# A retention layer and a two-layer MLP on one core: seven products also for block 5, and the whole order written down

## The chip, the core and the metric

The kernel runs on one core of a Trainium2 chip. A core has a matrix engine (TensorE, PE in the profile; PEld is its loading of weights), a vector engine (VectorE, DVE), a scalar engine with function tables (ScalarE, ACT), GpSimd (POOL) and SyncE (SP). Each takes its instructions in the order in which the program lists them and waits on semaphores for the others. Sixteen DMA engines move data; here POOL starts the loads, and SP starts the transposes of q and k and most stores. The metric is device time in microseconds (us) of one launch, the median of several runs; lower is better.

## The reference

```python
# q, k, v: (8 batches, 8 heads, 576 positions, 64)
scores = (1 / sqrt(64)) * q @ k.T
gamma  = 1 - 2.0 ** (-5 - arange(8))               # one per head
Dmat   = where(rel >= 0, gamma ** rel, 0)          # rel = query position - key position
x      = ((scores * Dmat) @ v)                     # no softmax
x      = x as (4608 tokens, 512 = heads * 64)
h      = x @ w_in                                  # (512, 2048)
g      = 0.5 * h * (1 + erf(h / sqrt(2)))          # exact gelu
out    = g @ w_out                                 # (2048, 512), float32
```

Products are made in bf16 with float32 sums.

## The kernel before

**Attention.** The work is cut into 36 units. A unit is 128 tokens: 128 positions (a chunk) of one batch with all heads, or, for the last 64 positions, both batches of a pair together. Units of one chunk and both batches of a pair form a group. There are 22 groups, numbered from 0: groups 0 to 3 are units 0 to 3, group 4 is units 4 and 5, group 5 is 6 and 7, group 6 is 8 and 9, group 7 is unit 10 (a short one), group 8 is 11 and 12, and so on. For each unit q, k and v are loaded by POOL (`load`, L322, which casts to bf16 on the way). q and k are turned: for groups 0 to 6 on TensorE (`turn`, L505), from group 7 on by DMA transposes from SP (`turn_dma`, L515). Then come the scores within the chunk (`scores`, L539, L548, L561), their masking on VectorE (`masked`), the product with v (`inner`, L636, L650), the running state of keys and values of earlier chunks (`state`, L669), the queries' product with that state (`cross`, L703), and the copy of the result, scaled by the decay, into the tile x of its block (`evacuate`). `scaled_v` scales v by its decay, on VectorE or ScalarE. These matmuls use halves and quarters of TensorE's array.

**MLP.** A block is 512 tokens, four units; there are nine, 0 to 8. In the first product (`mlp1`, L762) a block needs, for each of 16 slices of d_ff, four matmuls of 128x512. Gelu follows on ScalarE. Blocks 6 to 8 (`FAST = 6`) make the first product another way: `fast` (L1027) takes the 2 by 2 blocks of w_in and x and makes seven products of half size in place of eight (Winograd's form of Strassen's scheme). For each of four parts j of d_ff there are the products P1, P7, P6, P2, P5, P4, P3, each of four matmuls 128x256. They use sums of blocks of w_in (`sum_in`, `sum_last`; the latter writes over w_in, so only after the last plain `mlp1`), differences of blocks of x (`sum_x`), and results that are copied out of PSUM and added again on VectorE or ScalarE between the products: P6 and P2 need P1's copy, P5 and P4 need P6's sum, P3 needs P5's sum. The second product is plain in block 0 (`mlp2`, L807) and of seven products in blocks 1 to 8 (`part`, L946: M3, M4, M5, M1, M2, M6, M7, each in four steps, with the sums of gelu's result made by `sum_g` and those of w_out by `sum_w`).

**Order.** Everything is issued from one Python program, so the order of its calls is the order on each engine. A loop makes it. It keeps an estimate `T` of when each engine is free, and of when each load lands. At each turn it calls `fire`, which issues loads from the list `ORDER`, sums, casts, transposes and scaled v as their estimated times come. Then it chooses the next work for TensorE: cross product and evacuation, state, scores with the products that wait, a turn, or MLP work from `mlp_pick`. The rules are greedy: whatever is ready first. Entries of `ORDER` such as `s11+6` or `p31+20` shift the moment of single actions. While the loop has nothing for TensorE in the first 16 us, it issues filler matmuls on zeros (`warm`, L1241).

```python
        due = [a for a in acts if a[0] <= now]
        ...
        if pick and pick[0] <= now:
            one = pick[1].pop(0)
            ...
            {"1": mlp1, "2": mlp2, "3": part, "4": fast}[one[0]](*one[1:])
```

Copies that may run on either engine go through `either`, which takes the one that the estimate says is done sooner.

Of the kernel before, what the change touches and what calls it, by code (L numbers as in the profile page):

```python
# [9 lines left out]
FP32 = mybir.dt.float32  # L10
# [7 lines left out]
def kernel(  # L18
# [52 lines left out]
    FAST, ALL_FAST = 6, 6  # L71
# [23 lines left out]
    def x_of(i):  # L95
        t = i * C // TOK
        if t not in x_tiles:
            x_tiles[t] = x_pool.tile([128, N_DM, TOK], BF16, tag="xT", name="xT")
        return x_tiles[t][:, :, i * C % TOK:i * C % TOK + C]
# [157 lines left out]
    def sw_dma(issue, kind, put):  # L257
# [31 lines left out]
    def load(what, i):  # L289
# [17 lines left out]
        if what == "wo":  # L307
# [3 lines left out]
            queued.append((land_out[i] + 4.0, 3, sum_w, (i,)))  # L311
            return
        bp, ci, j = units[i]
        qk, v_ld = tiles_of(i)
        src = {"q": q, "k": k, "v": v}[what]
        for jj in (j,) if j is not None else range(2):
# [6 lines left out]
            if j is not None:  # L323
                sw_dma(0.94, "ld", putter(land, (what, i)))
            else:
                sw_dma(0.74, "short", putter(land, (what, i)))

    cast_due = {}
    for x, keys in enumerate(zip(*HW_FIRST)):
        for n, (what, i) in enumerate(keys):  # L330
# [3 lines left out]
    ORDER = ("wi1 k1 wi0 io q1 v0 q2 k2 v1 wi2 v2 k3 wi3 q3 v3 wi4 wi5 wi6 k4 q5 q4 q6 k5 v4 wi7 wo0 dq2 wo1 wo2 "  # L334
# [6 lines left out]
             "u3+0 u4+8 z12+0.3 p28+15 z15+1.6 z19+2.2 b18+4 p30+25 a19 p25+21 z23+2.2 u6+16 z6+0.3").split()  # L341

    BY_ACT = {int(x[1:]) for x in ORDER if x[0] == "a"}
    S_LATE = {int(x[1:].split("+")[0]): float(x.split("+")[1]) for x in ORDER if x[0] == "s"}
    B_LATE = {int(x[1:].split("+")[0]): float(x.split("+")[1]) for x in ORDER if x[0] == "b"}
    DVE_LAG, P_WAIT, HURRY = ({int(x[1:].split("+")[0]): float(x.split("+")[1]) for x in ORDER if x[0] == kind} for kind in "zpu")
    ORDER = [x for x in ORDER if x[0] not in "abszpu"]

    rest = const.tile([128, 2], BF16, name="rest")

    for n, g in enumerate(groups):
        ORDER += [what + str(i) for what in "qkv" for i in g if what + str(i) not in ORDER and (what, i) not in first]

    def v_free(i):
        return "Bdone" in st[i] if i in raw else "V" in st[i]

    def next_order():
        what = ORDER[0].rstrip("0123456789")
        n = int(ORDER[0][len(what):] or 0)
        if what == "h":  # L360
            if n >= nD:
                return False
            nc.gpsimd.tensor_copy(rest, qkT_of(n)[:, :, 0, 0])
            T["pool"] = max(T["pool"], sg[n]["T"]) + 0.2
        elif what in "qkv" and (group_of[n] >= next_load[0] or n >= 4 + N_V and not v_free(n - N_V)):
            return False
        else:
            load(what, n)
        ORDER.pop(0)
        return True  # L370
# [6 lines left out]

    next_load = [group_of[12] + 1]
    nD = N_PE_TR
    while T["pool"] < 4.0:  # L380
        next_order()

# [35 lines left out]
    def pe_waits(until):  # L418
        T["pe"] = max(T["pe"], until)
# [69 lines left out]
    def qkT_of(n):  # L489
        s = sg[n]  # L490
        if "qkT" not in s:
            if n < 4:
# [5 lines left out]
    def turn(n, jj, half):  # L498
# [8 lines left out]
        done = either(0.42 * rows / C, done, qkT[:, jj, HP * half:HP * half + HP, 0:rows], t[:, :, 0:rows])  # L507
# [3 lines left out]
    def turn_dma(n, jj):  # L511
# [10 lines left out]
        hw_dma(1.3, MOVE["turn"] * (0.62 if short else 1.0), max(land["qk"[jj], i] for i in groups[n]), put)  # L522

    def turnable(now):
        if nD >= len(groups) or nD >= group_of[min(nX, N_U - 1)] + N_QKT:
            return None
        return next((jj for jj in range(2) if jj not in sg[nD].get("ends", {})
                     and all(("qk"[jj], i) in land and land["qk"[jj], i] - 0.3 <= now for i in groups[nD])), None)

    def scores(n):  # L530
# [3 lines left out]
        if n < 4:  # L534
# [6 lines left out]
            st[g[0]]["sc"] = got, pe(0.23, H, "row")  # L541
            return
# [20 lines left out]
        done = pe(0.46, 4 * H, "quad")  # L563
        for j, i in enumerate(g):
            st[i]["sc"] = got[j], done

    def masked(i):
# [3 lines left out]
        (got, done) = s.pop("sc")  # L571
        if i < 4:
# [32 lines left out]
    def scaled_v(i):  # L605
# [3 lines left out]
        vh = vh_pool.tile([128, H, D], BF16, tag="vh", name="vh")  # L609
        at = land["v", i]  # L610
        by_act = i in BY_ACT
# [15 lines left out]
    def inner(i):  # L627
        bp, ci, j = units[i]
        s = st[i]
        pe_waits(max(s["R"], s["V"] if "vh" in s and i not in raw else land["v", i]))  # L630
# [22 lines left out]
        s["Bdone"] = True  # L653
        if j is None:
            s_done.add(i)
        elif j == 1 and ci < NCI - 1 and (bp, ci) != (1, 0):
            u_due.append((bp, ci))

    def state(bp, ci):
        pair = pair_of[bp, ci]  # L660
        assert (bp, ci) == (1, 0) or nX > (pair_of[bp, ci - 1] if ci else pair_of[bp - 1, NCI - 2] if bp else [-1])[-1]
# [16 lines left out]
        if pair[0] >= 4 and next_load[0] < len(groups):  # L678
            reload()
# [6 lines left out]

    def reload():
        next_load[0] += 1

    def cross(n):  # L690
# [14 lines left out]
        done = pe(0.2 if j0 is not None else 0.12, 2 * H, "quad")  # L705
        for i in g:
            st[i]["B"] = done

    def evacuate(i):
        bp, ci, j = units[i]  # L710
        s = st[i]
        if i in raw:
# [26 lines left out]
        if j is None and next_load[0] < len(groups):  # L739
            reload()  # L740
# [5 lines left out]

    def g_of(t, mm):
        return g_tiles[t, mm // 2][:, mm % 2] if t else g_tiles[t, mm // 2][mm % 2]

    def g_done(t, j):  # L750
        if t > 0 and all((t, 4 * j + x, ts) in g_at for x in range(4) for ts in range(4)):
            at = max(g_at[t, 4 * j + x, ts] for x in range(4) for ts in range(4)) - SEM
            for x in range(3):
                queued.append((at, x, sum_g, (t, j, x)))

    def mlp1(t, m0, n, lo, hi):
# [15 lines left out]
        done = on("act", 0.17 + n * (hi - lo) * 0.00084, done)  # L772
# [3 lines left out]
        g_done(t, m0 // 4)  # L776
# [23 lines left out]
    def mlp2(t, ts, m0, m1):  # L800
        cols = slice(ts * 128, ts * 128 + 128)
        if m0 == 0:
# [9 lines left out]
        if m1 == N_DF:  # L812
            if ts < 2:
# [25 lines left out]
    def sum_g(t, j, n):  # L839
# [8 lines left out]
        at = on("dve", 0.42 if n == 1 else 0.69, max(begun[x] for x in users_of(t - 1, j, n))) + SEM  # L848
# [7 lines left out]

# [552 lines left out]
```

## Time and profile before

| | |
|---|---|
| median of 3 runs | 286.22 us (286.12 to 286.31) |
| the profiled execution | 285.38 us |
| its span, first to last instruction | 283.6 us |
| TensorE busy | 276.4 us, 97% of the span |
| VectorE, ScalarE, POOL busy | 201.6, 144.2 and 114.2 us |
| granted TensorE clock | 1.0 throughout |
| chain that ended last | 88% TensorE |

A profile shows one execution. Its rows name a line of the kernel, an engine, an operation and tiles (out<-in). Waiting is told as idle time of an engine with the releaser that ended it. The chain is followed back from the last instruction: at each step to what released it, or to the instruction before it on its engine. Some records of matmuls are missing, a few in a hundred at most, so counts of matmuls in a row can be short by one or two.

### The profile page before, as it was taken

Reading aid. Unit: us, or ns where it says so; the run is one execution under the profiler, and the core shown is the slowest. Engines: PE = TensorE matmul, PEld = TensorE weight load, DVE = VectorE, ACT = ScalarE, POOL = GpSimd, SP = SyncE. Lnnn points to the kernel's source line nnn. Section 1 sums busy time; section 2 is a strip of 40 time slices with the busy share of each in tenths; the row PEclk is TensorE's granted clock in tenths of the full one; section 3 lists DMA queues with packets and bytes.
Section 4 is the critical chain, followed back from the end, with each engine's and each line's share of the span. In section 5 each row is a group of like instructions: output and inputs, shape, how many; then the busy total and the mean of one; then the engine's idle time right before and its main releaser. Section 6 shows DMA issues by size and latency. Waiting matters only on the chain.

```text
span 283.6 us, 8015 instructions
## 1 busy us (share of the span) xinstructions
PE 276.4 (97%) x3341; PEld 206.7 (73%) x3359; DVE 201.6 (71%) x395; ACT 144.2 (51%) x301; POOL 114.2 (40%) x143
## 2 busy tenths in 40 slices
PE   7999999999999999999999999999999999999994
PEld 2586577578874588457775687558888888888894
DVE  5743654959576765988549835899888779978732
ACT  5665635545456624696426524566655453545320
POOL 8988997994246484335548553000000000000000
PEclk9999999999999999999999999999999999999999
DMA  9999999999999999999999999960002100400133
GB/s 148 166 182 165 194 175 171 138 125 143 170 171 191 196 144 119 202 190 127 170 184 145 190 132 141 219 84 3 0 2 76 74 2 0 150 1 2 74 113 111
DMA packets 152804, 35.38 MB, mean 125 GB/s; under 512 B 141121, under 2 KB 148929, under 8 KB 152769
## 3 DMA queue, kind: packets, MB, share of 16 engines
q0 software_dynamic: 116832, 18.10, 97.0%
q1 hardware_dynamic: 34528, 16.26, 32.4%
q10 hardware_dynamic: 1408, 0.52, 0.8%
q8 instruction: 26, 0.43, 0.7%
q14 instruction: 10, 0.07, 0.1%
HBM read 36.70 MB, written 9.44 MB: 163 GB/s over the span
## 4 chain that ended last, share of the span: by engine, by line
PE 88%; POOL 6%; DMA 3%; issue 1%; DVE 1%; POOLq 0%
PE psum L946 35%; PE psum L762 26%; PE psum L1027 13%; PE psum L807 5%; DMA qk_ld<-in_q_dram 3%; PE psum L650 3%; PE psum L561 3%; POOL w_in L295 2%; POOL qk L322 2%; PE psum L669 1%; PE psum L703 1%; POOL v_ld L322 1%; PE psum L505 1%; POOL qk_ld L322 1%; PE psum L548 0%
## 5 line engine op out<-in xcount | busy, mean ns | idle before, releaser
L762 PE MATMUL psum<-xT,w_in 128*128 128x512 bf16 (+3 forms) x548 | 86.4, 311 | 1.0 <-issue 0.3
L771 ACT ACTIVATE g<-psum 128x512 bf16<-128x512 f32 (+2 forms) x106 | 58.3, 557 | 37.2 <-PE psum L762 35.4
L762 PEld LDWEIGHTS <-w_in 128*128 128x128 bf16 x560 | 48.5, 98 | 33.6 <-issue 0.5
L946 PEld LDWEIGHTS <-gs 128*128 128x128 bf16 x656 | 62.2, 98 | 7.8
L946 PE MATMUL psum<-w_sum,gs 128*128 128x256 bf16 (+1 forms) x400 | 48.3, 269 | 0.0
L322 POOL DMA_DIRECT2D v_ld<-in_v_dram x40 | 34.0, 858 | 16.6 <-DMA qk_ld<-in_k_dram 10.6
L322 POOL DMA_DIRECT2D qk_ld<-in_q_dram x36 | 30.5, 856 | 22.8 <-DMA qkT<-qk_ld 7.3
L322 POOL DMA_DIRECT2D qk_ld<-in_k_dram x36 | 30.5, 858 | 19.7 <-DMA qk_ld<-in_q_dram 19.4
L946 PE MATMUL psum<-w_out,gs 128*128 128x256 bf16 x256 | 32.7, 273 | 0.0
L946 PE MATMUL psum<-w_sum,g 128*128 128x256 bf16 x256 | 30.3, 273 | 0.0
L946 PEld LDWEIGHTS <-g 128*128 128x128 bf16 x256 | 24.8, 98 | 3.8
L1052 ACT ACTIVATE g<-psum 128x512 bf16<-128x512 f32 x36 | 20.4, 589 | 12.4 <-PE psum L1027 8.3
L593 DVE TENSOR_TENSOR ret<-psum,msk 128x1024 bf16<-128x1024 f32 x15 | 18.0, 1220 | 11.6 <-PE psum L561 4.7
L843 DVE TENSOR_TENSOR gs<-g 128x1024 bf16<-128x1024 bf16 x32 | 21.7, 685 | 5.3 <-ACT g L771 5.0
L847 DVE TENSOR_TENSOR gs<-g 128x1024 bf16<-128x1024 bf16 x32 | 21.4, 683 | 0.0
L1027 PEld LDWEIGHTS <-w_in 128*128 128x128 bf16 x192 | 18.7, 98 | 2.3
L898 DVE SCALAR_TENSOR_TENSOR o<-psum,o 128x512 f32<-128x512 f32 (+1 forms) x9 | 5.6, 630 | 19.4 <-PE psum L946 16.1
L617 DVE TENSOR_TENSOR vh<-v_ld,dv 128x512 bf16<-128x512 bf16 x28 | 18.4, 682 | 0.8 <-DMA v_ld<-in_v_dram 0.8
L484 ACT COPY o<-psum 128x512 f32<-128x512 f32 x13 | 7.6, 585 | 19.1 <-PE psum L946 19.1
L484 ACT CAST u_sb<-psum 128x512 bf16<-128x512 f32 x15 | 8.7, 586 | 15.8 <-PE psum L669 15.8
L614 ACT ACTIVATE vh<-v_ld,dv 128x64 bf16<-128x64 bf16 x64 | 16.1, 337 | 0.0
L1048 ACT ACTIVATE g<-p 128x512 bf16<-128x512 f32 x12 | 7.6, 630 | 16.1 <-DVE p L1046 16.1
(101 smaller groups left out, 357.1 us busy)
## 6 DMA issues: line engine op xcount, KB each, us to landing
out_dram<-o SPq DMA_DIRECT2D x27, 256.0 KB, 6.5
v_ld<-in_v_dram POOLq DMA_DIRECT2D x32, 128.0 KB, 9.8
qk_ld<-in_k_dram POOLq DMA_DIRECT2D x28, 128.0 KB, 9.6
qk_ld<-in_q_dram POOLq DMA_DIRECT2D x28, 128.0 KB, 8.8
w_in<-in_moe_w_in_dram POOLq DMA_DIRECT2D x8, 256.0 KB, 6.8
w_out<-in_moe_w_out_dram POOLq DMA_DIRECT2D x8, 256.0 KB, 7.6
out_dram<-o SPq DMA_DIRECT2D x14, 128.0 KB, 2.3
v_ld<-in_v_dram POOLq DMA_DIRECT2D x8, 64.0 KB, 8.5
```

The costliest lines, as they stand in the source:

```text
L322: nc.gpsimd.dma_start(dst, src[2 * bp + jj, :, ci * C:ci * C + n, :].rearrange("h s d -> s h d"))
L484: nc.scalar.copy(dst, src)
L593: nc.vector.tensor_tensor(r.rearrange("p e h q -> p (e h) q"), both_of(got[0][0], HP), by, op=ALU.mult)
L614: nc.scalar.activation(vh[:, h, :], loaded[i][1][:, h, :], AF.Copy, scale=dv[:, h, ci:ci + 1])
L617: nc.vector.tensor_tensor(vh, loaded[i][1], dv[:, :, ci:ci + 1].to_broadcast([128, H, D]), op=ALU.mult)
L762: nc.tensor.matmul(hT[:, m, :], lhsT=w[:, cc, o:o + 128], rhs=x_tiles[t][:, cc, lo:hi], start=(cc == 0), stop=(cc == N_DM - 1))
L771: nc.scalar.activation(g_of(t, m0 // 2)[:, m0 % 2:m0 % 2 + n, lo:hi], hT, AF.Gelu)
L843: nc.vector.tensor_tensor(s.rearrange("p m a b -> p m (a b)"), g[:, :, 0, :], g[:, :, 1, :], op=ALU.add)
L847: nc.vector.tensor_tensor(s, g[:, :, :, LEFT], g[:, :, :, RIGHT], op=MINUS)
L946: nc.tensor.matmul(m[:, 0 if apart else ts, :], lhsT=a, rhs=w[:, c0:c1], start=p in begins and mm == 0 and ts == 0, stop=mm == N_DF // 2 - ...
L1027: nc.tensor.matmul(m[:, y, :], lhsT=a[:, c], rhs=d[:, c], start=p in (P1, P7) and y == 0 and c == 0, stop=c == 1, skip_group_check=True)
L1052: nc.scalar.activation(g[:, :, rows, cols], m, AF.Gelu)
```

## The change

Blocks 5 to 8 now make the first product with seven products (`FAST = 5`). For blocks 5 and 6 the buffer of P7 is a tile in the place of the table `near` (decay factors, last read when unit 28's scores are masked); for blocks 7 and 8 it stays in a load buffer.

The greedy loop, `fire`, `mlp_pick` and the readiness rules are gone. A list `SEQ` of some 1,100 actions takes their place, each with its arguments: `L3.1` loads w_in1, `s7` makes the scores of group 7, `m10` masks unit 10, `f5.0.1` is block 5, part 0, second product (P7), `p4.3.1` is block 4, fourth of the seven second products, step 1, `G` is `sum_g`, `I`, `J` and `X` are the sums for the seven products, `d7.1` a DMA transpose of k, `v5.1` scaled v on ScalarE. A loop performs them in turn. The list was recorded from a run of such rules and then changed by a search that moves single actions. The estimate `T` still exists: it decides in `either`, and the functions now note more of the times at which buffers come free.

```diff
-    FAST, ALL_FAST = 6, 6
+    FAST, ALL_FAST = 5, 5
...
-    ORDER = ("wi1 k1 wi0 io q1 v0 q2 k2 v1 wi2 v2 k3 wi3 q3 v3 wi4 wi5 wi6 k4 q5 q4 q6 k5 v4 wi7 wo0 dq2 wo1 wo2 "
-             "v5 dq3 wo3 k7 k6 k8 q9 wo5 wo7 dq4 v7 q7 wo4 v6 wo6 k9 q11 v11 q8 v10 q12 k10 v9 v8 q10 k12 k11 v12 "
...
-    def scaled_v(i):
+    def scaled_v(i, by_act):
...
+    near_p7 = True
+    def late_p7(t):
+        return not near_p7 or t >= N_BLK - 2
...
         elif p == P7:
-            if not p7_tiles:
-                p7_tiles.append(ld_pool.tile([128, 2, 2, 256], FP32, tag="qk", bufs=N_LD, name="p7"))
-            f_bank[key, "p7"] = p7_tiles[0][:, j % 2]
-            at = either(0.68, done, f_bank[key, "p7"], m)
+            late = t >= N_BLK - 2
+            if late not in p7_tiles:
+                more = {"tag": "qk", "bufs": N_LD} if late else {"tag": "near"}
+                p7_tiles[late] = (ld_pool if late else const).tile([128, 2, 2, 256], FP32, name="p7", **more)
+            f_bank[key, "p7"] = p7_tiles[late][:, j % 2]
+            at = either(0.68, max(done, p7_free(t, j)), f_bank[key, "p7"], m)
...
-    while True:
-        fire()
-        now = T["pe"]
...
+    SEQ = ("L3.1 L1.1 L3.0 L5.0 L0.1 L2.0 L0.2 L1.2 C0.0 C1.0 t0.0.0 Z0 w2 L2.1 Z0 Z1 t0.1.0 Z0 w5 L3.2 Z1 s0 m0 L2.2 Z1 "
+           "w7 L1.3 Z1 t1.0.0 L3.3 Z1 t1.1.0 w2 Z1 i0 L0.3 Z1 v0.0 x0 e0 w2 s1 m1 L2.3 t2.0.0 10.0.2.0.128 L3.4 t2.1.0 "
+           "10.2.2.0.128 L3.5 i1 x1 e1 w1 L3.6 s2 m2 10.4.2.0.128 L1.4 10.0.2.128.256 x3 10.2.2.128.256 10.4.2.128.256 "
+           "v1.0 u0.0 x2 i2 e2 10.6.2.0.256 t3.0.0 t3.1.0 10.2.2.256.384 10.6.2.256.384 10.0.2.256.384 L3.7 10.9.1.0.384 "
+           "10.8.1.0.384 s3 m3 10.10.1.0.384 10.11.1.0.384 10.12.1.0.384 L1.5 L0.5 i3 L0.4 10.13.1.0.384 10.15.1.0.384 e3 "
...
+           "11.12.2.256.512 d8.1 11.14.2.256.512 d7.0 d8.0 11.10.2.256.512 L0.14 G1.0.1.2 K K G1.0.1.0 v8.0 i8 u1.0 d9.0 "
+           "G1.0.1.1 i9 u0.3 x6 s7 m10 e8 p1.0.0 p1.0.1 G1.1.1.0 G1.2.1.1 p1.1.0 p1.0.2 p1.0.3 p1.1.1 L1.15 L1.13 L1.14 "
...
+           "G3.2.1.2 13.13.1.0.512 v21.0 G3.1.1.0 G3.2.1.0 13.14.1.0.512 i20 i21 G3.2.1.1 G3.3.1.1 u2.1 x13 e20 p3.0.0 I4 "
...
+           "p4.0.3 p4.1.0 G4.2.1.1 v28.1 p4.1.1 p4.1.2 G4.3.1.0 p4.1.3 p4.2.0 L0.32 p4.2.1 p4.2.2 J6 X5 p4.3.0 J7 G4.3.1.1 "
+           "p4.2.3 d19.0 f5.0.0 p4.3.1 f5.0.1 e26 L2.29 L0.33 p4.3.2 p4.3.3 f5.0.2 p4.4.0 f5.0.3 p4.4.1 f5.0.4 L1.34 L0.34 "
...
+           "p8.5.0 p8.5.1 p8.5.2 p8.5.3 p8.6.0 p8.6.1 p8.6.2 p8.6.3").split()
...
+    for x in SEQ:
+        perform(x[0], [int(y) for y in x[1:].split(".") if y])
```

More of the change, by code (lines that the diff above doesn't have):

```diff
@@ L255, with qk_free, sw_dma @@
     w_in_sb, w_out_sb, land_in, land_out = {}, {}, {}, {}
-    def sw_dma(issue, kind, put):
+    ld_ring, v_ring, vh_ring, ret_ring, qkT_ring = [], [], [], [], []
+    def qk_free(n):
+        g = groups[n]
+        ends = list(sg[n]["ends"].values()) if "ends" in sg[n] else [sg[n]["T"]]
+        assert len(ends) == 2 or n < N_PE_TR and sg[n]["halves"] == 4
+        assert units[g[0]][2] is None or g[0] in s_done
+        return max(ends + [st[g[0]].get("U", 0.0)])
+    def sw_dma(issue, kind, put, ready=0.0):
+        T["pool"] = max(T["pool"], ready)
         if len(flying) >= 8:
@@ L333, with constant @@
             cast_due[what, i] = (t[1] if what == "v" else t[0][:, "qk".index(what)], first[what, i])
-    ORDER = ("wi1 k1 wi0 io q1 v0 q2 k2 v1 wi2 v2 k3 wi3 q3 v3 wi4 wi5 wi6 k4 q5 q4 q6 k5 v4 wi7 wo0 dq2 wo1 wo2 "
[6 rows of a table removed]
[L341 to L347, printed above, removed]
-    rest = const.tile([128, 2], BF16, name="rest")
[L351 to L370, printed above, removed]
+    rest = const.tile([128, 2], BF16, name="rest")
+    def constant(n):
+        at, engine, dur, fn = later.pop(n)
+        fn()
+        on(engine, dur, at)
     def finish_later():
@@ L506, in turn @@
         done = pe(0.225, HP)
[L507 removed]
+        sg[n]["halves"] = sg[n].get("halves", 0) + 1
+        done = either(0.42 * rows / C, max(done, sg[n]["Q"]), qkT[:, jj, HP * half:HP * half + HP, 0:rows], t[:, :, 0:rows])
         release(b, done + 0.05)
@@ L520, in put @@
             sg[n]["T"] = max(ends.values()) + SEM
[L522 to L528, printed above, removed]
+        hw_dma(1.3, MOVE["turn"] * (0.62 if short else 1.0), max([sg[n]["Q"]] + [land["qk"[jj], i] for i in groups[n]]), put)
     def scores(n):
@@ L745, with g_free @@
     acc = {}
+    def g_free(t, j):
+        if t < 2 or t == N_BLK - 1:
+            return 0.0
+        return max([begun[t - 1, M3, j], begun[t - 1, M4, j]] + [gs_at[t - 1, 2 * j, n] for n in range(3)])
     def g_of(t, mm):
         return g_tiles[t, mm // 2][:, mm % 2] if t else g_tiles[t, mm // 2][mm % 2]
[L750 to L754, printed above, removed]
     def mlp1(t, m0, n, lo, hi):
@@ L932, in part @@
         if p == M3 and k == 0:
+            assert t == 1 or (t - 1, M7, 3) in begun
+            assert t != N_BLK - 2 or nX == N_U and all(f_step.get((x, y)) == 6 for x in range(FAST, t) for y in range(4))
             for x in range(2):
@@ L993, in sum_last @@
         wi_at[mm, 1] = on("dve", 0.28, max(wi_at[mm, 0], wi_read[mm])) + SEM
+    f_end = {}
     def sum_x(t):
+        assert t == FAST or all(f_step.get((t - 1, j)) == 6 for j in range(0, N_DF // 4, 1 + (t - 1 < ALL_FAST)))
         x = x_tiles[t]
@@ L1382 @@
+    for x in SEQ:
+        perform(x[0], [int(y) for y in x[1:].split(".") if y])
+    assert nX == N_U and all((t, 6, 3) in begun for t in range(1, N_BLK))
 _INS = ['q', 'k', 'v', 'moe_w_in', 'moe_w_out']
```

395 lines of the change are left out of this document (87 added, 308 removed), and 57 rows, old and new, of tables (ORDER, SEQ).

## The prediction

> **What bounds the kernel now.** I read the page first: totals, clock and DMA rows, and the chain that ended last.
>
> ```profile
> span 283.6 us, 8015 instructions
> ...
> PE 276.4 (97%) x3341; PEld 206.7 (73%) x3359; DVE 201.6 (71%) x395; ACT 144.2 (51%) x301; POOL 114.2 (40%) x143
> ...
> PEclk9999999999999999999999999999999999999999
> DMA  9999999999999999999999999960002100400133
> ...
> PE 88%; POOL 6%; DMA 3%; issue 1%; DVE 1%; POOLq 0%
> ```
>
> TensorE is busy for 97% of the span at full clock, and 88% of the chain is its own. The DMA engines are full for 26 slices, some 184 us, but with POOL they hold only 9% of the chain. The table of stretches shows where TensorE is not full.
>
> ```profile
> 0.00:28.00 28.00, 25.78 (x292) 16.53 (x295) 15.37 (x51) 17.04 (x40) 24.83 (x36) 1.00 1.82 165
> 28.00:168.00 140.00, 138.79 (x1823) 96.98 (x1835) 100.57 (x189) 72.15 (x155) 85.12 (x102) 1.00 1.95 164
> 168.00:252.00 84.00, 83.90 (x963) 68.22 (x964) 67.25 (x121) 45.15 (x89) 4.29 (x7) 1.00 0.48 67
> ```
>
> The first number after the length is TensorE's busy time, the third VectorE's. After 28 us TensorE lacks 1.2 us of 140 and 0.1 of 84. So time is won by giving TensorE less to do, by a better start, or out of about 1 us of waits. Being busy includes the pipeline's depth, so a matmul's price is taken from the chain, where each row has start, length and count:
>
> ```profile
> 27.36 1.34 PE psum L762 x24
> ...
> 32.52 3.45 PE psum L807 x16
> ...
> 38.98 6.11 PE psum L762 x56
> ```
>
> These are 128, 512 and 256 columns wide: 1.34/24 = 55.8 ns, 3.45/16 = 215.6 ns, 6.11/56 = 109.1 ns.
>
> **The change part by part.** *Seven products for block 5.* In the order of instructions on TensorE (it has no times) 64 matmuls of 512 columns give way to 112 of 256: 64 x 215.6 = 13.80 us against 112 x 109.1 = 12.22 us, -1.58 us on the path. Two narrow ones cost 2 x 109.1 - 215.6 = 2.6 ns more than a wide one, which is in the sum.
>
> The Trainium skill, "TensorEngine Tiling (Array Packing)", section Instruction Overhead, speaks against the change: it gives each matmul about 60 cycles of overhead. At the 2.4 GHz of its page "TensorE: Matmul & The Clock Gate" (table at the top) that is 25 ns, an estimate of 1.2 us for 48 more matmuls, and the sum below would be a loss of 0.4 us. The trace's 2.6 ns disagree.
>
> *What VectorE and ScalarE get for it.*
>
> ```profile
> L1042 DVE TENSOR_TENSOR psum<-p,psum 128x512 f32<-128x512 f32 x12 | 8.3, 694 | 3.4 <-PE psum L1027 1.8 <-ACT p L484 1.4
> L1046 DVE TENSOR_TENSOR p<-p,psum 128x512 f32<-128x512 f32 x12 | 8.2, 682 | 2.0 <-PE psum L1027 2.0
> ...
> L479 DVE COPY psum<-psum 128x512 f32<-128x512 f32 x8 | 5.6, 697 | 1.5 <-PE psum L1027 1.4
> ...
> L1000 DVE TENSOR_TENSOR xs<-xT,xs 128x512 bf16<-128x512 bf16 x6 | 2.5, 420 | 0.1
> ```
>
> Both counts of 12 become 16: 4 x (0.694 + 0.682) = 5.5 us. Block 5's four input differences add 4 x 0.42 = 1.7 us. Eight more results are copied out, on VectorE at 0.697 each or on ScalarE: 0 to 5.6 us. That is 7.2 to 12.8 us more for VectorE around block 5, where it is now busy 67.25 of 84 us (80%); with 82.4 us left it would be 90 to 97%. The cover is TensorE's other work: between a product and the one that needs its copy lie 0.9 us of other matmuls at the least, mostly 1.3 us or more, in both orders. Without cover a late link costs up to one operation, 0.69 us. I take nothing, since 80% cost TensorE 0.1 us, and keep three late links, 2.1 us, for the range. Gelu stays at sixteen 512-wide activations for the block. The sums of w_in are made a block earlier, where VectorE is busy 100.57 of 140 us; the last differences, which overwrite w_in, still follow block 4's last read and precede the first product. P7's buffer moves to the tile of decay factors, free long before. Nothing for each of these.
>
> *Changes of array shape.* Attention uses halves and quarters of the array.
>
> ```profile
> L669 PE MATMUL psum<-vh,qk_ld 128*64 128x64 bf16 x224 | 5.9, 196 | 0.0
> ```
> ```profile
> 200.46 0.42 PE L669 MATMUL psum<-vh,qk_ld 128*64 128x64 bf16 x16
> 200.81 0.38 PE L548 MATMUL psum<-qkT 64*64 64x64 bf16 x12
> ```
>
> The last of the 16 starts at 200.46 + 0.42 - 0.196 = 200.68, 15 ns apart from the one before, and the next shape starts at 200.81: 0.11 us lost. The recorded list has 80 such changes, the kernel before 75; behind the point used next, 68 and 64: +0.44 us.
>
> *The start.* The first 18 loads stand in the same order on POOL's queue. TensorE turns q of unit 3 as it lands:
>
> ```profile
> 11.75 0.97 POOL L322 DMA_DIRECT2D qk<-in_q_dram  x1
> ...
> 15.69 1.01 POOL L322 DMA_DIRECT2D qk_ld<-in_k_dram  x1
> ```
> ```profile
> qk<-in_q_dram POOLq DMA_DIRECT2D x1, 128.0 KB, 7.1
> ```
> ```profile
> qk_ld<-in_k_dram POOLq DMA_DIRECT2D x1, 128.0 KB, 9.1
> ```
> ```profile
> 18.93 0.62 PE L505 MATMUL psum<-ident,qk 128*128 128x128 bf16 x8
> ...
> 26.75 0.61 PE L505 MATMUL psum<-ident,qk_ld 128*128 128x128 bf16 x8 [0.18 <-DMA qk_ld<-in_q_dram]
> ```
>
> 11.75 + 7.1 = 18.85, and the turn starts at 18.93. So what TensorE does ahead of this point is free, and what is left behind it counts. Ahead of it the list has two fillers fewer (of 512 zeros) and eight matmuls of 128 columns fewer; these eight now come behind: 8 x 55.8 ns = +0.45 us. Behind it w_in7 moves ahead of three loads of units 4 and 5, next after k of unit 4, which lands at 15.69 + 9.1 = 24.8. With 1.3 us for its 256 KB (an estimate from the wider spacing of such loads here) it lands near 26.1. TensorE, with 6.2 us of matmuls and four changes of shape since the turn, would come to it at 25.5: 0.6 us of waiting, where the kernel before waits 0.2 us for q of unit 4 at 26.75. Against the 0.4 us stand the other waits of before, 0.8 us by the check below, which this order need not repeat. I take nothing net, with the ends -0.3 and +0.5.
>
> *SP's queue.* Unit 10's second transpose was second on SP and becomes third, behind one of units 11 and 12; unit 10's scores on TensorE wait for it, and all matmuls behind them. The second and third of before, and those scores:
>
> ```profile
> L515 SPq DMA_TRANSPOSE qkT<-qk_ld x1: 1201/1201/1201, 57.3 to 57.3; - x1
> ...
> DMA to landing us min/median/max: 7.5/7.5/7.5
> ```
> ```profile
> L515 SPq DMA_TRANSPOSE qkT<-qk_ld x1: 1246/1246/1246, 58.7 to 58.7; - x1
> ...
> DMA to landing us min/median/max: 9.8/9.8/9.8
> ```
> ```profile
> L548 PE MATMUL psum<-qkT x16: 192/193/213, 65.4 to 65.7; 64*64 64x64 bf16 x16
> ```
>
> They landed at 64.8 and 68.5. In the list the loads ahead are one fewer (some 0.9 us), so the third should land near 67.6. Up to these scores the list has 2.45 us more matmuls and two changes of shape fewer: TensorE comes at 65.4 + 2.45 - 0.22 = 67.6. Nothing, with 0.8 us kept for the range; a gain is excluded, since a transpose cannot hurry matmuls that stand later. Later groups of scores stand within 1.5 us of their old place up to block 4; the last four stand 14 to 30 us later, which gives loads, transposes and the queues behind them time.
>
> *The end* keeps its order: last products, differences, stores.
>
> ```profile
> 276.23 3.68 PE L946 MATMUL psum<-w_sum,gs 128*128 128x256 bf16 x40
> ```
>
> *The sum.* -1.58 + 0.45 + 0.44 = -0.7 us. Check: matmuls behind the turn at these prices 252.9 us and 64 changes 7.0 us, from 18.93, give 278.9; the last matmul ends at 276.23 + 3.68 = 279.9. So 1.0 us of waits lie behind it, and without any the sum would be -1.7 us. The profiled execution took 285.4 us, 1.8 more than its span; the median of the runs is 286.2. -0.7 us gives 284.7 on the profiled execution and 285.5 on the median.
>
> **The rivals.** *The list also loses the waits.* All actions were moved about, so most of the 1.0 us may go: 284.7. Against it: the kernel before was already without waits from 168 us on, so only the DMA-fed part can give.
>
> *No change: the DMA keeps the pace.* Unit 10's third place on SP costs its 0.8 us, or the loads of the first 30 us do; the gain is spent waiting: 286.3. For it: DMA full for 184 us; scores that started 0.6 us after their transpose. The fixed cost per matmul doubted above would also end near here, 286.6, and 2.6 ns leave it 1 in 100.
>
> *Slower: VectorE becomes the bound from block 5 to 8.* At 97% a queue in fixed order has no room; a late copy of a product stops TensorE, with all that is behind it. From 1.3 us of lateness (two links of 0.69) the result is slower by over 0.2%; three links give 286.2 - 0.7 + 2.1 = 287.6, two 286.9, and I write 287.2. Against it: ScalarE is busy 45.15 of 84 us there and takes copies.
>
> **How the numbers follow.** My forecast 285.5 has 0.50 (its own range 285.0 to 286.0), the lost waits 0.10, no change 0.20, VectorE 0.20. 0.2% is 0.57 us, about what a measurement tells from nothing. Of the forecast's 0.50 I count 0.40 as faster and 0.10 within; of no change 0.15 within and 0.05 slower; of VectorE 0.02 within and 0.18 slower. Faster 0.50, within 0.27, slower 0.23. The range goes from 284.3, nearly all waits gone, to 287.2, the VectorE case.
>
> **What would show it.** Right: L762 with 64 wide matmuls fewer and the seven-product line with 448; the turn of unit 3 near 18.9; unit 10's scores at 67 to 68; TensorE still at 83.8 or more in each 84 us behind 168. Wrong: TensorE idle ahead of unit 10's scores with a DMA as releaser (no change); VectorE over 90% with TensorE gaps ended by its copies (slower); the last matmul before 278.5 (waits gone).

## The result and the profile after

The changed kernel takes 284.51 us (median of 22 runs), the kernel before 285.70 us (22 runs beside them): a ratio of 0.9962, 95% interval 0.9946 to 0.9979, or 1.2 us less. The forecast was 0.7 us less, its range reached 1.9 us less.

The totals of the page, and the table of stretches with the columns of the prediction:

```profile
span 282.3 us, 8187 instructions
...
PE 276.3 (98%) x3413; PEld 211.7 (75%) x3413; DVE 211.3 (75%) x413; ACT 152.6 (54%) x330; POOL 114.1 (40%) x143
...
PE 91%; POOL 4%; DMA 3%; issue 0%; DVE 0%; POOLq 0%
```
```profile
0.00:28.00 28.00, 25.65 (x274) 15.52 (x275) 14.47 (x48) 17.39 (x40) 23.66 (x35) 1.00 1.73 168
28.00:168.00 140.00, 140.00 (x1866) 98.68 (x1864) 108.20 (x210) 74.19 (x164) 84.85 (x102) 1.00 2.03 163
168.00:252.00 84.00, 84.00 (x1020) 73.66 (x1019) 71.83 (x122) 52.58 (x113) 5.56 (x7) 1.00 0.50 69
```

Behind 28 us TensorE is never idle. (Of the 1.2 us that it lacked between 28 and 168 us before, about 1.0 were missing records: there were 3341 of matmuls and 3359 of weight loads, and the gaps stand at L762 and L807, where records are missing; here both are 3413.) The whole list of TensorE's waits is four lines, with total, times and longest; the one behind the turn of unit 3 is the last. Then TensorE's timeline around it, and the end of the chain:

```profile
PE psum L1106 <- DVE zeros L119: 1.2, 1, 1.2
PE psum L499 <- DMA qk<-in_q_dram: 0.7, 1, 0.7
PE psum L672 <- DVE vh L617: 0.2, 1, 0.2
PE psum L762 <- DMA w_in<-in_moe_w_in_dram: 0.2, 1, 0.2
```
```profile
18.87 0.61 PE L499 MATMUL psum<-ident,qk 128*128 128x128 bf16 x8
19.32 1.50 PE L762 MATMUL psum<-xT,w_in 128*128 128x128 bf16 x24
21.05 1.47 PE L762 MATMUL psum<-xT,w_in 128*128 128x384 bf16 x8 [0.24 <-DMA w_in<-in_moe_w_in_dram]
```
```profile
263.31 15.34 PE psum L948 x156
```

From the turn of unit 3 to the end of the last matmul are now 263.31 + 15.34 - 18.87 = 259.8 us; before they were 261.0. Of these -1.2 us the prediction's terms are -1.58 + 0.45 + 0.44 = -0.7. The other 0.5 us are waits, by the same reckoning: the prediction's check sum left 1.0 us of them before (252.9 us of matmuls and 64 changes of shape against 261.0); the same sum with 251.8 us and 68 changes leaves 0.5 us now. Four tenths of that stand in one place: the 24 matmuls from 19.32 should end at 20.66 by the chain's 55.8 ns each, and the next starts at 21.05.

### The profile page after: what moved, and what is told of

It reads as the page before. It is cut to its first block, busy times and chain, and to the rows that moved or that the text cites. A ratio compares the mean times of both kernels' runs of the same rounds, so it can differ in the third digit from the quotient of the medians.

```text
span 282.3 us, 8187 instructions
## 1 busy us (share of the span) xinstructions
PE 276.3 (98%) x3413; PEld 211.7 (75%) x3413; DVE 211.3 (75%) x413; ACT 152.6 (54%) x330; POOL 114.1 (40%) x143
## 4 chain that ended last, share of the span: by engine, by line
PE 91%; POOL 4%; DMA 3%; issue 0%; DVE 0%; POOLq 0%
PE psum L948 35%; PE psum L762 23%; PE psum L1047 18%; PE psum L807 5%; PE psum L651 3%; PE psum L551 3%; DMA w_in<-in_moe_w_in_dram 3%; POOL qk L347 2%; PE psum L702 2%; PE psum L672 1%; POOL v_ld L347 1%; POOL w_in L306 1%; PE psum L499 1%; PE psum L538 0%; PE psum L637 0%
## 5 line engine op out<-in xcount | busy, mean ns | idle before, releaser
L762 PE MATMUL psum<-xT,w_in 128*128 128x512 bf16 (+3 forms) x504 | 74.1, 301 | 0.3 <-DMA w_in<-in_moe_w_in_dram 0.2
L771 ACT ACTIVATE g<-psum 128x512 bf16<-128x512 f32 (+2 forms) x91 | 49.6, 546 | 31.6 <-PE psum L762 27.2
L762 PEld LDWEIGHTS <-w_in 128*128 128x128 bf16 x504 | 42.6, 98 | 25.0 <-DMA w_in<-in_moe_w_in_dram 0.9
L948 PE MATMUL psum<-w_sum,gs 128*128 128x256 bf16 (+1 forms) x400 | 50.5, 268 | 0.0
L1074 ACT ACTIVATE g<-psum 128x512 bf16<-128x512 f32 x48 | 27.0, 593 | 7.5 <-PE psum L1047 6.5
L614 ACT ACTIVATE vh<-v_ld,dv 128x64 bf16<-128x64 bf16 x88 | 22.0, 336 | 0.0
L1047 PEld LDWEIGHTS <-wi 128*128 128x128 bf16 x192 | 18.5, 98 | 2.4 <-issue 0.2
L1047 PE MATMUL psum<-xT,w_in 128*128 128x256 bf16 x128 | 19.2, 273 | 0.0
L1047 PE MATMUL psum<-xs,w_in 128*128 128x256 bf16 x128 | 18.9, 273 | 0.0
L1047 PE MATMUL psum<-xs,wi 128*128 128x256 bf16 x128 | 18.7, 273 | 0.0
L1070 ACT ACTIVATE g<-p 128x512 bf16<-128x512 f32 x16 | 10.1, 630 | 13.9 <-DVE p L1068 13.9
```

The lines of the kernel that those rows point to most:

```text
L614: nc.scalar.activation(vh[:, h, :], loaded[i][1][:, h, :], AF.Copy, scale=dv[:, h, ci:ci + 1])
L762: nc.tensor.matmul(hT[:, m, :], lhsT=w[:, cc, o:o + 128], rhs=x_tiles[t][:, cc, lo:hi], start=(cc == 0), stop=(cc == N_DM - 1))
L771: nc.scalar.activation(g_of(t, m0 // 2)[:, m0 % 2:m0 % 2 + n, lo:hi], hT, AF.Gelu)
L948: nc.tensor.matmul(m[:, 0 if apart else ts, :], lhsT=a, rhs=w[:, c0:c1], start=p in begins and mm == 0 and ts == 0, stop=mm == N_DF // 2 - ...
L1047: nc.tensor.matmul(m[:, y, :], lhsT=a[:, c], rhs=d[:, c], start=p in (P1, P7) and y == 0 and c == 0, stop=c == 1, skip_group_check=True)
L1070: nc.scalar.activation(g[:, :, 1, RIGHT], v, AF.Gelu)
```

## The experiments

**Seven products undone, inside the list.** The list keeps its other moves; at every second product of block 5 stands a plain slice, and the last sums of w_in go back behind block 5.

```diff
-    FAST, ALL_FAST = 5, 5
+    FAST, ALL_FAST = 6, 6
-           ... d19.0 f5.0.0 p4.3.1 f5.0.1 e26 L2.29 L0.33 p4.3.2 p4.3.3 f5.0.2 p4.4.0 f5.0.3 ...
+           ... d19.0 15.0.1.0.512 p4.3.1 e26 L2.29 L0.33 p4.3.2 p4.3.3 15.1.1.0.512 p4.4.0 ...
```

> The recorded list with block 5's first product plain again: at the places of the first, third, fifth and seventh product of each part stands one plain slice of four 512-column matmuls, the differences of block 5 are gone, and the last differences of w_in follow block 5. TensorE gets 64 x 215.6 - 112 x 109.1 ns = 1.58 us more and as many changes of array shape. Theory (the seven products are wholly on the path in this list): 1.6 us slower than the changed kernel, 286.1 us on 284.5, which is 0.4 us above the kernel before, ratio 1.001. Rival (VectorE's and ScalarE's added work ate a part of it): VectorE is freed here, so at most 1.0 us slower, 285.5 us or less, ratio 0.999 or less. Rival (the list's other moves are what won): below 285.0.

Measured: 286.73 us, ratio to before 1.0023 (1.0008 to 1.0037). Against the changed kernel's 0.9962 that is 0.6% or 1.7 us. The profiled execution says the same and shows a part that isn't the products: from the turn at 19.08 us to the end of the last matmul it takes 261.4 us, 1.6 more than the changed kernel. The waits are no fewer: the one at w_in4 is gone, since this execution came to the turn 0.2 us later, and my edit made another, because the last sums of w_in now stand next to a mask on VectorE.

```profile
19.08 0.51 PE L499 MATMUL psum<-ident,qk 128*128 128x128 bf16 x6 [0.41 <-DMA qk<-in_q_dram]
```
```profile
192.85 0.60 PE L1047 MATMUL psum<-xs,w_in 128*128 128x256 bf16 x4 [0.32 <-DVE ret L588]
```
```profile
265.11 15.34 PE psum L948 x156
```

So the seven products are worth about what the sum gave them, as the expectation had it. Without them the list is no faster than the greedy order: it is 0.2% slower.

**Seven products alone, under the greedy rules.** The kernel before, with P7's buffer for blocks 5 and 6 in the tile of decay factors.

```diff
-    FAST, ALL_FAST = 6, 6
+    FAST, ALL_FAST = 5, 5
...
-            if not p7_tiles:
-                p7_tiles.append(ld_pool.tile([128, 2, 2, 256], FP32, tag="qk", bufs=N_LD, name="p7"))
-            f_bank[key, "p7"] = p7_tiles[0][:, j % 2]
+            late = t >= N_BLK - 2
+            if late not in p7_tiles:
+                more = {"tag": "qk", "bufs": N_LD} if late else {"tag": "near"}
+                p7_tiles[late] = (ld_pool if late else const).tile([128, 2, 2, 256], FP32, name="p7", **more)
+            f_bank[key, "p7"] = p7_tiles[late][:, j % 2]
```

> The kernel before, with its greedy rules, and only the seven products for block 5 added (P7's buffer for blocks 5 and 6 in the tile of decay factors). TensorE's matmuls behind the turn of unit 3 get 1.58 us shorter, and the rules leave 69 changes of array shape in place of 64, 5 x 0.11 = 0.55 us. Theory (VectorE is covered also without a list made for it): 1.58 - 0.55 = 1.0 us faster than before, ratio 0.9964, TensorE busy at 83.8 or more in each 84 us behind 168. Rival (the added VectorE work needs an order that was made for it): TensorE idles ahead of products of block 5 with VectorE or ScalarE copies as releasers, 0.69 us for each late link; from two of them on it is no faster than before, ratio 1.000 or more.

Measured: 290.44 us, ratio 1.0151 (1.0125 to 1.0176): 4.3 us slower than before, where the same products make the list faster. TensorE's largest waits behind the start and the stretch behind 168 us, then VectorE's timeline at the first large gap:

```profile
PE psum L1027 <- DVE p L1048: 1.1, 1, 1.1
PE psum L946 <- DVE psum L887: 0.9, 1, 0.9
PE psum L946 <- DVE gs L843: 0.9, 1, 0.9
PE psum L505 <- DMA qk_ld<-in_q_dram: 0.9, 1, 0.9
```
```profile
168.00:252.00 84.00, 79.89 (x972) 68.53 (x971) 70.40 (x122) 44.59 (x90) 3.61 (x6) 1.00 0.48 66
```
```profile
188.59 1.23 DVE L593 TENSOR_TENSOR ret<-psum,msk 128x1024 bf16<-128x1024 f32 x1 [0.23 <-PE psum L561]
189.73 1.28 DVE L601 TENSOR_TENSOR ret<-psum,msk 128x512 bf16<-128x512 f32 x2
190.92 1.28 DVE L617 TENSOR_TENSOR vh<-v_ld,dv 128x512 bf16<-128x512 bf16 x2
192.12 0.68 DVE L843 TENSOR_TENSOR gs<-g 128x1024 bf16<-128x1024 bf16 x1
...
193.66 0.69 DVE L887 TENSOR_TENSOR psum<-o,psum 128x512 f32<-128x512 f32 x1
```

VectorE is busy 70.4 of 84 us here, less than in the changed kernel (71.8), and TensorE waits for it all the same: two masks and two scaled v, 3.5 us without a break, stand in its queue ahead of three sums of gelu's result (L843 is the first) and the addition (L887) for which TensorE waits here. At 220.7 us two more masks and scaled v stand ahead of the sum (L843) for which it waits 0.9 us. The share of a long stretch doesn't tell late from early; what is queued ahead of the one operation does.

**The copies of P1 and P7 by force.** In the changed kernel `either` puts 14 of these 32 copies on VectorE and 18 on ScalarE, six of the 18 in block 5. Three kernels change only this (the estimate is kept, so that nothing else moves); the edit of the first is shown, the second has it for block 5 alone, the third with `nc.scalar.copy`.

```diff
+    def on_dve(fast_dve, ready, dst, src):
+        nc.vector.tensor_copy(dst, src)
+        if max(T["dve"], ready) + fast_dve <= max(T["act"], ready) + 0.6:
+            return on("dve", fast_dve, ready)
+        return on("act", 0.6, ready)
...
-            at = either(0.68, done, to[1], m)
+            at = on_dve(0.68, done, to[1], m)
...
-            at = either(0.68, max(done, p7_free(t, j)), f_bank[key, "p7"], m)
+            at = on_dve(0.68, max(done, p7_free(t, j)), f_bank[key, "p7"], m)
```

> The changed kernel with all 32 copies of P1 and P7 in blocks 5 to 8 on VectorE (18 of them run on ScalarE in the changed kernel); nothing else is moved. 18 x 0.69 = 12.4 us more for VectorE: from 71.8 of 84 us between 168 and 252 us to about 82, 97%. Theory (each copy has 0.9 us or more of other matmuls as cover and the queue catches up): at most 0.3 us slower than the changed kernel. Rival (at 97% a queue in fixed order has no room): two to three late links of 0.69 us, 1.4 to 2.1 us slower, TensorE idle ahead of products with copies as releasers.

> The changed kernel with the eight copies of P1 and P7 of block 5 all on VectorE (six of them run on ScalarE in the changed kernel); blocks 6 to 8 as they are. 6 x 0.69 = 4.1 us more for VectorE, all between 166 and 185 us. Theory (what counts is how much VectorE work is queued ahead of the one copy that a product needs, and the list leaves room only where it put it): late links as in the run with all copies on VectorE, which had 1.1 us of TensorE waiting at 181 us and 1.0 us at 193 us: 1.1 to 2.1 us slower than the changed kernel. Rival (what counts is VectorE's share over a long stretch; 71.8 + 4.1 of 84 us is 90%): at most 0.3 us slower.

> The changed kernel with all 32 copies of P1 and P7 on ScalarE (14 of them run on VectorE in the changed kernel). VectorE loses 14 x 0.69 = 9.7 us, ScalarE gets 14 x 0.58 = 8.1 us: from 52.6 of 84 us between 168 and 252 us to about 60, 71%. Theory (VectorE's queue is the tight one): within 0.3 us of the changed kernel. Rival (each copy's engine was chosen where that engine is free, so any other choice makes late links): 1 us slower or more, with ScalarE copies as releasers ahead of products.

Measured: all on VectorE 290.48 us, ratio 1.0159 (1.0135 to 1.0183), 5.6 us slower than the changed kernel by the ratios; block 5's on VectorE 285.52 us, ratio 0.9983 (0.9965 to 1.0001), 0.6 us slower, with intervals that overlap a little, between the two expectations; all on ScalarE 285.15 us, ratio 0.9972 (0.9959 to 0.9985), 0.3 us slower, which the intervals don't tell from nothing and the theory allowed (its longest new wait, 0.7 us, has a copy on ScalarE as releaser). The stretch from 168 us of each, in this order:

```profile
168.00:252.00 84.00, 79.56 (x970) 68.73 (x968) 75.87 (x130) 40.11 (x90) 5.56 (x7) 1.00 0.52 70
```
```profile
168.00:252.00 84.00, 83.23 (x1011) 72.66 (x1009) 74.82 (x129) 49.24 (x107) 4.87 (x6) 1.00 0.53 68
```
```profile
168.00:252.00 84.00, 83.31 (x1013) 72.86 (x1011) 64.89 (x111) 56.41 (x122) 5.55 (x7) 1.00 0.60 70
```

The rival of the first run was right in kind and far too small: not two or three late links but waits all the way through blocks 5 to 8. VectorE never came to the 97% that I worked out, because TensorE slowed down with it: it stands at 75.9 of 84 us. With block 5's copies alone there is one late place. TensorE's and VectorE's timelines there, and below them ScalarE's in the changed kernel, where the same copy (`COPY psum`) stands:

```profile
180.82 0.60 PE L1053 MATMUL psum<-xs,w_in 128*128 128x256 bf16 x4
181.58 0.60 PE L1053 MATMUL psum<-xs,wi 128*128 128x256 bf16 x4 [0.16 <-DVE psum L1070]
182.78 0.60 PE L1053 MATMUL psum<-xs,wi 128*128 128x256 bf16 x4 [0.61 <-DVE psum L480]
```
```profile
180.83 0.70 DVE L1070 TENSOR_TENSOR psum<-p,psum 128x512 f32<-128x512 f32 x1
181.43 0.69 DVE L855 TENSOR_TENSOR gs<-g 128x1024 bf16<-128x1024 bf16 x1
182.04 0.69 DVE L480 COPY psum<-psum 128x512 f32<-128x512 f32 x1
```
```profile
180.52 0.57 ACT L474 COPY psum<-psum 128x512 f32<-128x512 f32 x1 [0.28 <-DVE gs L845]
```

TensorE's order is the same in both, and so is the cover of other matmuls between a product and its user. The copy is that of P1 of part 3, whose matmuls start at 179.51 here and at 179.89 in the changed kernel. On VectorE it stands behind an addition and a sum and begins at 182.04, 2.5 us after its product's start; on ScalarE it began at 180.52, 0.6 us after it. The 0.3 and 0.8 us by which TensorE's rows lie too far apart there (four matmuls take 0.44) are the whole of this kernel's new waiting; at w_in4 it waits about 0.2 us less than the changed kernel.

**The greedy rules with all copies on ScalarE.** The same edit with `nc.scalar.copy` in the second kernel, and the estimate told so.

> The greedy rules with seven products for block 5, and all 32 copies of P1 and P7 on ScalarE (18 run on VectorE in the run of the greedy rules before this one, which had 6.9 us of TensorE waiting). 18 x 0.69 = 12.4 us less for VectorE. Theory (the greedy order loses because VectorE's queue is late for the products): the waiting falls to 3 us or less, ratio 1.002 or less. Rival (the greedy order is late elsewhere: sums of gelu's results, masks, ScalarE): 6 us or more of waiting stay, ratio 1.012 or more.

Measured: 287.57 us, ratio 1.0052 (1.0032 to 1.0072). It lies between the two expectations: of the loss against before about two thirds are gone, and by the check sum 5.0 us of waits stay. One part of what stays is not VectorE's at all, the others still are:

```profile
PE psum L509 <- DMA qk_ld<-in_q_dram: 1.4, 1, 1.4
...
PE psum L1031 <- DVE p L1052: 1.1, 1, 1.1
PE psum L1031 <- DVE ret L597: 0.4, 1, 0.4
```

The first is q of unit 4, for which TensorE waited 0.18 us in the profile before and 0.9 us in the greedy run above, with the same matmuls and loads in the same order up to there. Three profiles of one start, and this wait differs by over 1 us; the list has other work at that place.

**The loads of the start.** Two entries of the list are moved, so that w_in4 and w_in7 start earlier.

```diff
-           ... w2 s1 m1 L2.3 t2.0.0 10.0.2.0.128 L3.4 t2.1.0 ... m2 10.4.2.0.128 L1.4 ... 10.0.2.256.384 L3.7 10.9.1.0.384
+           ... w2 s1 m1 t2.0.0 10.0.2.0.128 L3.4 t2.1.0 ... m2 10.4.2.0.128 L2.3 L3.7 L1.4 ... 10.0.2.256.384 10.9.1.0.384
```

> The changed kernel with two loads of the start moved in POOL's order: v of unit 3 behind w_in4 to w_in6, and w_in7 ahead of k of unit 4. w_in4 lands a load earlier, near 20.0 in place of 21.0, and w_in7 near 24.9 in place of 25.9. In the changed kernel TensorE waits 0.24 us at w_in4, the longest wait behind the turn of unit 3. Theory (this landing, not the turn of unit 3, is the last thing of the start that TensorE waits for): 0.3 to 0.4 us faster than the changed kernel, first matmul with w_in4 at 20.7. Rival (something else lands or is copied just in time behind it): no change, and a new wait of 0.2 to 0.4 us behind 21 us, at w_in5, w_in6 or unit 3's product with v.

Measured: 284.18 us, ratio 0.9947 (0.9924 to 0.9970), which is not told from the changed kernel's 0.9962. The wait at w_in4 is gone (32 matmuls follow each other from 19.38; the row names the first shape only, the last eight are 384 columns wide), and another has come in:

```profile
18.93 0.62 PE L499 MATMUL psum<-ident,qk 128*128 128x128 bf16 x8 [0.39 <-DMA qk<-in_q_dram]
19.38 2.80 PE L762 MATMUL psum<-xT,w_in 128*128 128x128 bf16 x32
```
```profile
95.89 0.64 PE L551 MATMUL psum<-qkT 64*64 64x128 bf16 x32 [0.29 <-DMA qkT<-qk_ld]
```

0.4 us are won at 20 us, 0.3 are lost at 95 us to a transpose that landed just in time before: the second expectation, at a place that I hadn't named.

**More changes of shape.** Six actions of the list, of four full-array matmuls each, are moved forward into groups of attention matmuls (the expectation says seven; two of the moves took the same action); one of them:

```diff
-           ... i15 i16 u1.3 x10 s11 L2.19 p2.3.0 p2.3.1 ...
+           ... i15 i16 p2.3.0 u1.3 x10 s11 L2.19 p2.3.1 ...
```

> The changed kernel with seven steps of second or first products (four full-array matmuls each, or one slice) moved forward into groups of attention matmuls, so that TensorE changes the shape of its array 80 times behind the turn of unit 3 in place of 68; the matmuls are the same. Theory (a change of shape costs TensorE about 0.11 us wherever it stands): 12 x 0.11 = 1.3 us slower than the changed kernel, span 283.6 us on 282.3. Rival (the cost shows between the records but is mostly gone in the sum, since weights are loaded in that time): at most 0.4 us slower.

Measured: 285.71 us, ratio 0.9987 (0.9966 to 1.0008), 0.7 us slower than the changed kernel by the ratios, span 283.9 us. Its profiled execution came to the turn of unit 3 half a microsecond late, for a load; the same lateness took the wait at w_in4 away:

```profile
18.50 1.05 PE L762 MATMUL psum<-xT,w_in 128*128 128x256 bf16 x8 [1.29 <-DMA w_in<-in_moe_w_in_dram]
19.38 0.61 PE L499 MATMUL psum<-ident,qk 128*128 128x128 bf16 x8
```
```profile
264.82 15.34 PE psum L948 x156
```

From that turn to the end are 260.8 us, 1.0 more than in the changed kernel, with 0.4 us less of waiting: 12 changes cost 1.4 us, 0.12 us each. The theory's price holds; the times alone would not have shown it.

**Lists changed further.** Three kernels were to use what VectorE has left: the changed kernel's list after another search of local moves on its own estimate, then seven products for block 4 too (one v buffer fewer, a P7 buffer of half the size, a list from the same search), and that once more with a search that left the start alone and allowed for later transposes.

```diff
-    FAST, ALL_FAST = 5, 5
+    FAST, ALL_FAST = 4, 4
...
-    N_V = 9
+    N_V = 8
...
+    p7_first = const.tile([128, 2, 256], FP32, name="p7_first")
...
+            if t == FAST:
+                f_bank[key, "p7"] = p7_first
-            if late not in p7_tiles:
+            elif late not in p7_tiles:
```

> The changed kernel's own work with its list changed further: from the turn of unit 3 on, single actions of all engines were moved by a local search on the kernel's own estimate of when each engine is free. The same matmuls, 67 changes of array shape behind the turn in place of 68. Theory (after the changed kernel's 0.5 us of waits there is nothing left to win by order): 0.5 us faster at most, span 281.8 us or more on 282.3. Rival (the order still holds 1 us or more, as the search's estimate says): span 281.3 us or less.

> Seven products for block 4 too (one buffer fewer for v, P7 of block 4 in a buffer of its own of half the size), with a list made by the same search. Again 64 matmuls of 512 columns give way to 112 of 256: -1.58 us; 70 changes of array shape in place of 68: +0.22; waits as in the changed kernel or 0.5 us fewer. VectorE gets another 7.2 us or more between 140 and 165 us. Theory (with copies and sums placed by the search VectorE has room for one block more): 1.4 to 1.9 us faster than the changed kernel, span 280.4 to 280.9 us. Rival (VectorE is late in blocks 3 and 4, where masks, sums of w_in and of gelu's results stand as well): TensorE waits of 1 us or more behind 120 us with VectorE as releaser, span 282 us or more.

> Seven products for block 4 too, as in the run before this one, with a list whose search left the first 71 actions alone, kept the sums of w_in at least 100 actions behind the late stores of block 0, and counted the mean of three estimates, two of them with later DMA transposes. -1.58 us of matmuls, 74 changes of array shape in place of 68: +0.66. Theory (what was lost in the run before were transposes and loads of the start, not VectorE): with 0.5 us of waits as in the changed kernel 0.9 us faster than it, span 281.4 us, ratio to before 0.993. Rival (any list moved this far has new waits for DMA that the estimate doesn't see): waits of 1.5 us or more, span 282.3 us or more, ratio 0.996 or more.

Measured: 298.95 us, ratio 1.0428 (1.0387 to 1.0468); 286.77 us, 1.0035 (1.0006 to 1.0064); 290.26 us, 1.0147 (1.0121 to 1.0174). All three are slower than the changed kernel, the first by 14 us, though the estimate of each was 1.2 to 1.9 us lower than the changed kernel's. Neither expectation of the first had a loss in mind; both of the second were wrong, since its large waits are for DMA and not for VectorE; of the third the rival held, new waits for DMA. The chain of the first shows the main reason (start, length):

```profile
117.18 9.22 DMA out_dram<-o
...
126.42 0.30 DVE wi L991
...
127.28 0.69 DVE xT L736
...
128.02 0.91 PE psum L551 x23
```

The sums of w_in are written into the tiles that hold block 0's results until they are stored. The search had moved a late store and these sums close together; VectorE stood still until the store had landed, and TensorE, waiting for banks behind an evacuation, with it. The estimate doesn't know this dependency; in the changed kernel 139 of the list's 977 actions lie between. In the second and third the largest waits are for transposes; the second's stretch of block 4, and its wait at group 17's scores:

```profile
120.00:162.00 42.00, 42.00 (x570) 32.49 (x569) 39.03 (x74) 27.26 (x63) 25.15 (x30) 1.00 2.22 170
```
```profile
164.82 0.36 PE L551 MATMUL psum<-qkT 64*64 64x128 bf16 x12 [2.48 <-DMA qkT<-qk_ld]
```

VectorE was busy for 39.0 of 42 us, 93%, and TensorE was never idle: there was room for block 4's products on VectorE. What was missing was the transfer, which landed 11.5 us after its start. The third had two such waits, 4.2 us together.

The stops are not the whole loss. At the end of TensorE's stop of 2.5 us at 162.8 us the third's granted clock fell to 0.5 for 3.4 us, and matmuls of 256 columns there start 213 ns apart in place of 109. The second's stop of nearly the same length and place left its clock at 1.0 in the profiled execution. The twelve matmuls of `part` that follow the stop, in the third and in the second, and the clock of the first in 40 slices:

```profile
166.72 2.37 PE L948 MATMUL psum<-w_sum,g 128*128 128x256 bf16 x12
```
```profile
165.65 1.48 PE L948 MATMUL psum<-w_sum,g 128*128 128x256 bf16 x12
```
```profile
PEclk9999999999988999969999999999999999999998
```

In the first the clock was 0.5 twice, from 87.5 us for 3.4 us (a stop of 2.3 us ended at 86.6) and from 125.0 us for 6.8 us (the stop of 6.0 us began at 122.0). TensorE worked for 7.2 us of these; half of that, 3.6 of the 14 us, is an estimate of what the clock cost there, and 1.7 us in the third.

So the order of the changed kernel isn't shown to be the best one, but none of these is better, and whether seven products for more blocks would pay stays open.

## Why the prediction was right, and where it was not

*Seven products, -1.58.* Right: undoing them costs 1.6 us in the trace and 1.7 us by the ratios. The fixed cost per matmul that I doubted is out. With the 25 ns of the Trainium skill ("TensorEngine Tiling (Array Packing)", Instruction Overhead) added to each matmul, undoing them would have cost 0.4 us; the runs here disagree with that reading (two matmuls of 256 columns cost 2.6 ns more than one of 512). The section's own example is of matmuls of 1 and of 60 columns, which take equally long; no matmul here is that narrow, so no run here shows it.

*VectorE and ScalarE, taken at nothing.* The value was right, the reason for it was not. VectorE's total rose by 9.7 us (201.6 to 211.3), inside the 7.2 to 12.8, but partly by luck: of the copies of P1 and P7 it makes 14 in place of 15, and about 3 us are work that I hadn't counted, copies of results and of x among it. Its share didn't reach 90 to 97%: it is 71.8 of 84 us, 85%, since ScalarE got 18 of the 32 copies (45.2 to 52.6 us) and only 4.6 of the 9.7 us fall into this stretch. But I named as cover the 0.9 us or more of other matmuls between a product and its user "in both orders". This cover was the same in the kernel with block 5's copies on VectorE, and TensorE waited 1.1 us. And the greedy order, which I had counted as one of the two with cover, loses 5.6 us of waits behind 180 us (6.9 in all by the check sum, less the 1.3 before) on the same products. What covers a copy is not its distance from the user but that distance less everything ahead of it in the queue of the engine that makes it. The bound of three late links, 2.1 us, was as wrong: with VectorE late, waits came to 5.6 us there and to about 6.5 with all copies on VectorE. The rival "VectorE becomes the bound" got its chance for a wrong measure, too. 84% of VectorE with 4 us of TensorE idle (greedy) stand against 93% with none (block 4 above). The recorded list is what made this step come out: it has the copies where their engine is free. My reading couldn't tell the two orders apart, so it was luck that the value came out right.

*Shapes, +0.44.* Right: 0.11 to 0.12 us each, also where twelve more were put in.

*The start, +0.45 and nothing net.* The sum was right (the turn at 18.87, predicted near 18.9). The wait came at another load. w_in7, issued at 16.93, landed after 8.9 us, at 25.86, as TensorE came to it (its first matmul there starts at 25.91, at most 0.06 us late). TensorE had been held up at w_in4, which I had passed over: issued at 13.50, landed after 7.5 us, at 21.0, for a TensorE that was ready at 20.7.

```profile
L306 POOL DMA_DIRECT2D w_in<-in_moe_w_in_dram x1: 845/845/845, 13.5 to 13.5; - x1
...
DMA to landing us min/median/max: 7.5/7.5/7.5
```

*Unit 10's transpose.* The scores start at 67.46 (predicted 67.6) and wait for nothing, but not as worked out. The third transpose on SP, started at 58.1, landed after 6.6 us, at 64.7, not 67.6. I had given it the 9.8 us of the one that was third before; the time from issue to landing doesn't go with the place in the queue.

```profile
L510 SPq DMA_TRANSPOSE qkT<-qk_ld x1: 1318/1318/1318, 58.1 to 58.1; - x1
...
DMA to landing us min/median/max: 6.6/6.6/6.6
```
```profile
67.46 0.42 PE L538 MATMUL psum<-qkT 64*64 64x64 bf16 x16
```

*The waits.* This is the term that was off: I took the 1.0 us of before as unchanged, with a tenth for all of it going. Half went: the forecast of -0.7 became -1.2, between the forecast and the rival "the list also loses the waits" (-1.7 by its sum); the last matmul ended at 278.6, just above the 278.5 that I had named as this rival's sign. The check sum that showed the 1.0 us was a better guide than my reading of where they were: the 1.2 us that TensorE seemed to lack between 28 and 168 us were mostly missing records, and the largest wait, q of unit 4, was 0.2 to 1.4 us in three executions of the greedy start. Reckoned as w_in4 above, it cost 0.34 us before (11 matmuls from 25.80 end at 26.41, the turn starts at 26.75), and w_in4 costs 0.39 now: the start kept its wait, at another load, so the half that went lies in smaller waits behind it. Which of these gave how much isn't settled by these runs.

## What to carry to other kernels

Before you call added work on a second engine covered, list what stands ahead of it in that engine's queue at that moment, and subtract it from the distance to the user; the engine's share of a long stretch decides nothing. An arithmetic saving on the bound engine and the order that makes room for it are one change: here each alone was slower than before, and together they were faster. Where an order is written by a search on an estimate, what the estimate leaves out (a buffer that waits for a store, a transpose that lands late) is what the next search will spend; and a stop of the bound engine can cost more than its length, as the clock of the two lists above shows.

## What the runs showed of the hardware

The cost of changing the array's shape depends on the direction: in the profile after it is 0.09 us from the full array to halves or quarters, 0.11 from halves to quarters, 0.12 from halves and 0.12 to 0.13 from quarters back to the full array (medians of the distance between the starts of neighbouring matmuls, less the mean cadence of the first). And between 52 and 70 us the DMA transposes from SP landed 5.9 to 7.6 us after their start in the changed kernel and 7.4 to 11.3 us before, a difference that no term of mine had. At the end of one stop of TensorE of 2.5 us, 0.9 us behind one of 2.3 us, and during one of 6.0 us, the granted clock fell to 0.5 for 3.4 us or longer; behind another of 2.5 us it did not, and no stop shorter than 2.3 us behind the start is followed by such a fall in these profiles.
